# Attention and mixture of experts on one core: router logits in the spare columns of the scores' bank, and other engines for weights and token halves

## The chip, the cores and the metric

The kernel runs on one core of one Trainium2 chip. The metric is the device time of one execution in microseconds (us), and lower is better. A core has a matrix engine (TensorE, "PE" in the rows; "PEld" is its loading of stationary operands), VectorE (DVE), ScalarE (ACT), GpSimd (POOL) and SyncE (SP), which here does nothing but issue transfers. Each engine has its own queue of instructions and works through it in order; a transfer runs on 16 DMA engines that all queues share.

## The reference

Attention inside blocks of 64 tokens makes `x`, 4608 tokens of 512 numbers. Tokens whose skip score is positive go through one of eight experts, the one with the largest logit; the others leave unchanged.

```python
scores = (1 / np.sqrt(D)) * np.matmul(q_c, k_c.transpose(0, 1, 2, 4, 3))   # blocks of 64 tokens
attn = np.exp(scores - scores.max(-1, keepdims=True))
attn = attn / (attn.sum(-1, keepdims=True) + 1e-09)
x = np.matmul(attn, v_c)                       # reordered to (4608, 512)
do_compute = (x @ w_skip) > 0
xc = x[do_compute]
logits = xc @ w_gate                           # 8 experts
e_idx = np.argmax(logits, axis=1)
gate_w = softmax(logits)[e_idx]
for e in range(8):
    h = np.maximum(xc[e_idx == e] @ w1[e], 0.0)        # 512 -> 1024
    y[e_idx == e] = gate_w * (h @ w2[e])               # 1024 -> 512
out = x; out[do_compute] = xc + y
```

## The kernel before, in words

The program has two stages. The first takes 36 tiles of 128 tokens through attention and the router. The second takes the tokens of each expert, gathered from `out`, through the two matrix products of that expert; the expert that is first in the order has its weights loaded and converted already during the first stage, in 16 halves ("pieces") of 128 x 512 numbers.

The first stage is one loop over `i`, and its order is written out by hand: in pass `i` different steps of different tiles stand one behind the other on each engine. On TensorE a pass is: transpose `x` of tile i-3 into the bank `xt` (`pe_xtrans`), transpose the exponentials of tile i-1 (`pt`), subtract the maxima of tile i (`pe_sub`), logits of tile i-4 (`pe_logits`), scores of tile i+1 (`pe_scores`, tile `sp`), product with v of tile i-1 (`pv`). On ScalarE: scale `xt` to `xs` (line 300), copy `pt` to `pts` (257), exponential `px` (245). On VectorE: normalise `pv` to `x` (273 to 277), sum the logits (`lg`, 326), maxima (`mx`, 235), then some steps of the router of a finished group of tiles (`run_route`, groups of 14, 9 and 13 tiles).

Before the logits, `xs` is split into two half-precision parts, the tile `xh`: the high part is a copy (line 302), the low part what the copy left (line 303), both on GpSimd. The logits of a tile are written into columns of the same bank `xt` that `pe_xtrans` of this pass has filled (`rt_bank`, the list `host`), so they come behind the ScalarE step that empties it. For the last five tiles ScalarE and VectorE make `xh` straight from the bank.

`conv_half` converts one piece of weights: ScalarE makes the high part in `wset` (475), GpSimd scales the staged piece `wst` in place (479) and subtracts (480). It is called at the end of a pass, once the piece has been in flight for two passes.

Transfers are issued in bursts. TensorE's instructions are counted, and whenever a block of 256 (`FETCH`) has gone by, SP issues one burst: first `qk` and `v` of tiles up to four ahead, then, until the burst has 6 units (7 from pass `WIDER` on; `qk` counts two, all others one), pieces of weights that `W_TILES` makes due and stores of finished `x` (`held`). A piece or a store is 128 x 512 x 4 bytes, 262,144 bytes.

When the router is through with the first 23 tiles, GpSimd gathers the rows of the first three blocks of the first expert (`early_fetch`, at the end of pass `EARLY_I`). After the loop TensorE finishes the last tiles' logits between the first products of that expert (tile `pd`), and goes on to the second products (`y`) and the other experts.

Of the kernel before, what the change touches and what calls it, by code (L numbers as in the profile page):

```python
# [9 lines left out]
F32 = mybir.dt.float32  # L10
F16 = mybir.dt.float16
# [3 lines left out]
ALU = mybir.AluOpType  # L15
# [3 lines left out]
P = 128  # L19
B, H, S, D = 8, 8, 576, 64  # L20
CH = 64
NTOK = B * S
NT = NTOK // P
DM = H * D
# [3 lines left out]
KC = DM // P  # L28
# [9 lines left out]
GS = (14, 9, 13)  # L38
NG = len(GS)
GT = [(g, i, n) for g, n in enumerate(GS) for i in range(n)]  # L40
EARLY_G, EARLY_B = 2, 3
# [8 lines left out]
FETCH_AT = 193  # L50
FETCH_LAG = 12
BURST = 6
WIDER = 18
W_TILES = (6, 8, 11, 14, 17, 20, 23, 25, 33, 33, 33, 33, 34, 34, 34, 34)
W_ORDER = tuple((fc, part) for part in range(2) for fc in range(FC))
WSETS = 3
STB = 8
# [1 line left out]
XGB = 8  # L59
TLEAD = 2  # L60
XBUFS = 17
EARLY_I = NT - 3

SX = 2.0 ** 6
SW = 2.0 ** 4
# [36 lines left out]
def moe_attention_kernel(ctx: ExitStack, tc: tile.TileContext, qk: bass.AP, v: bass.AP, cst: bass.AP, wall: bass.AP, out: bass.AP):  # L102
    nc = tc.nc
# [7 lines left out]
    ap = apool.__enter__()  # L111
# [3 lines left out]
    ps_s = spool_.__enter__()  # L115
# [4 lines left out]
    T = [dict() for _ in range(NT)]  # L120
# [13 lines left out]
    def mm32(*args, **kw):  # L134
        return issued(nc.tensor.matmul(*args, **kw), 4)  # L135
# [69 lines left out]
    def more_constants():  # L205
        nc.vector.tensor_copy(upper, C("upper"))
        nc.vector.tensor_copy(iota, C("iota"))
        nc.vector.tensor_scalar(wgs[:, :, 0], wg, SR, None, op0=ALU.mult)
        nc.vector.scalar_tensor_tensor(wgs[:, :, 1], wg, SR, wgs[:, :, 0], op0=ALU.mult, op1=ALU.subtract)
        nc.gpsimd.tensor_copy(vals[:, :, 0], C("tok"))  # L210
        nc.gpsimd.tensor_copy(vals[:, :, 2], C("part").to_broadcast([P, NT]))
        nc.gpsimd.memset(ecum[:, 0, :], 0.0)
        nc.gpsimd.memset(rec, 0.0)
# [7 lines left out]

    def pe_scores(t):
        qt = T[t].pop("qk")
        sp = ps_s.tile([P, 2, DM], F32, name="sp")
        for j in range(KC):
            for c in range(2):
                for a in range(2):
                    h = (j % 2) * 4 + (j // 2) * 2 + a
                    w = slice(h * CH, (h + 1) * CH)
                    mm32(sp[halves[a], c, j * CH:(j + 1) * CH], qt[halves[c], 0, w], qt[halves[c], 1, w], start=(j == 0), stop=False, skip_group_check=True)  # L230
        T[t]["sp"] = sp

    def ve_max(t):
        mx = spool.tile([P, H], BF16, name="mx")
# [45 lines left out]
    held = []  # L280
# [11 lines left out]
    def ac_xs(t):  # L292
        if t >= NT - 5:
            T[t]["xh"] = xh = ap.tile([P, 2, KC, P], F16, name="xh")
            xp = T[t].pop("xt")
            nc.scalar.activation(xh[:, 0], xp, AF.Copy, scale=SX)
            nc.vector.scalar_tensor_tensor(xh[:, 1], xp, SX, xh[:, 0], op0=ALU.mult, op1=ALU.subtract)
            return
        xs = ap.tile([P, KC, P], F32, name="xs")
        nc.scalar.activation(xs, T[t].pop("xt"), AF.Copy, scale=SX)  # L300
        T[t]["xh"] = xh = ap.tile([P, 2, KC, P], F16, name="xh")
        nc.gpsimd.tensor_copy(xh[:, 0], xs)  # L302
        nc.gpsimd.tensor_tensor(xh[:, 1], xs, xh[:, 0], op=ALU.subtract)  # L303

    host = []

    def rt_bank():
        if not host:
            host.append(ps_p.tile([P, DM], F32, name="xt"))
        return host[0]  # L310

    def pe_logits(t):
        xh = T[t].pop("xh")
        lp = rt_bank()[:, :2 * NX]
        for j in range(KC):
            mm16(lp, xh[:, 0, j, :], wgs[:, j].rearrange("p z n -> p (z n)"), start=(j == 0), stop=False, skip_group_check=True)
            mm16(lp[:, :NX], xh[:, 1, j, :], wgs[:, j, 0], start=False, stop=(j == KC - 1), skip_group_check=True)
        T[t]["lp"] = lp
# [14 lines left out]
    def route(g):  # L333
# [36 lines left out]

        yield "p", 0
        rk = rt_bank()[:, 32:32 + n * NX]
        mm16(rk, upper, eh.rearrange("p g e -> p (g e)"), start=True, stop=False, skip_group_check=True)
        for i in range(1, n):
# [45 lines left out]
        yield "w", 1  # L420
        yield "p", 0
        rp = rt_bank()[:, 32:32 + 4 * NB]
        for i in range(n):
            mm16(rp, oh[:, i, :], rv[:, i].rearrange("p z b -> p (z b)"), start=(i == 0), stop=(i == n - 1), skip_group_check=True)
# [27 lines left out]
    def run_route(kinds, budget):  # L452
        while routes and routes[0][0][0] in kinds and budget > 0:
            budget -= routes[0][0][1]
            routes[0][0] = next(routes[0][1], None)
            if routes[0][0] is None:
                routes.pop(0)
# [13 lines left out]
    def conv_half(eng=nc.gpsimd):  # L471
        st, fc, r = w_pend.pop(0)
        loaded.pop(0)
        w = wsets[0]
        nc.scalar.activation(w[:, 0, fc, r], st, AF.Copy, scale=SW)
        if eng is nc.vector:
            eng.scalar_tensor_tensor(w[:, 1, fc, r], st, SW, w[:, 0, fc, r], op0=ALU.mult, op1=ALU.subtract)
        else:
            eng.tensor_scalar(st, st, SW, 1.0, op0=ALU.mult, op1=ALU.mult)
            eng.tensor_tensor(w[:, 1, fc, r], st, w[:, 0, fc, r], op=ALU.subtract)  # L480
# [66 lines left out]
    def on(f, t, *a):  # L547
        if 0 <= t < NT:
            f(t, *a)
# [19 lines left out]
    def early_fetch():  # L569
        for m in range(min(EARLY_B, ready[-1])):  # L570
            fetch(m, P * sum(GS[:EARLY_G]))
# [48 lines left out]
    ahead = [f for t in range(4, NT + 1) for f in ([(load_qk, t, 2)] if t < NT else []) + [(load_v, t - 1, 1)]]  # L620
    pieces = list(range(len(W_TILES)))

    def burst(at):
        i, size, put = now[0], 0, []
        while ahead and ahead[0][1] <= i + LOOK and size + ahead[0][2] <= BURST:
            put.append(ahead.pop(0))
            size += put[-1][2]
        while size < BURST + (i >= WIDER):
            if pieces and W_TILES[pieces[0]] <= i:
                put.append((load_half, pieces.pop(0), 1))  # L630
            elif held:
                put.append((store, held.pop(0), 1))
            else:
                break
            size += 1
        for n, (f, t, _) in enumerate(put):
            f(t, None if n else at)

    pe["burst"] = burst
    for i in range(-1, NT):  # L640
        host.clear()
        now[0] = i
        pe["n"] += 1
        run_route("w", 1)
        on(pe_xtrans, i - 3)
        on(ve_norm, i - 2)
        on(ac_xs, i - 3)
        if 0 <= i - 2 < NT:
            held.append(i - 2)
        on(pe_ptrans, i - 1)  # L650
        on(ac_pt, i - 1)
        on(pe_sub, i)
        on(ac_exp, i)
        on(pe_logits, i - 4)
        run_route("p", 1)
        on(ve_logits, i - 4)
        run_route("r", 1)
        on(pe_scores, i + 1)
        on(ve_max, i + 1)
        run_route("d", 750)  # L660
        on(pe_pv, i - 1)
        if i == 1:
            more_constants()
        for _ in range(2 if i == NT - 1 else 1):
            if not w_pend or i < loaded[0] + (2 if i < EARLY_I else 1):
                break
            conv_half()
        while i == EARLY_I and len(ready) == 1:
            host.clear()
            run_route("w", 1)  # L670
            run_route("p", 1)
            run_route("rd", 1 << 30)
        if i == EARLY_I:
            early_fetch()
# [17 lines left out]
    while held:  # L692
        store(held.pop(0))
    store(NT - 2)
    ac_xs(NT - 3)
    pe_logits(NT - 4)
    ve_logits(NT - 4)
# [8 lines left out]
    piece()  # L706
    pe_xtrans(NT - 2, pt_bank)
    ac_xs(NT - 2)
    pe_logits(NT - 3)
    ve_logits(NT - 3)  # L710
# [245 lines left out]
```

## Time and profile before

| | us |
|---|---|
| median of 3 runs (lowest, highest) | 354.51 (353.32, 357.58) |
| the profiled execution | 354.38 |
| its span, first to last instruction | 352.7 |
| TensorE busy | 315.1 (89%) |
| VectorE busy | 237.8 (67%) |
| ScalarE busy | 164.4 (47%) |
| GpSimd busy | 149.2 (42%) |

The mean granted clock of TensorE is 0.982 of 2.4 GHz. The loop over the tiles takes up the first 130 us of the span. The shares are means over both stages; the engines' loads differ much between them, so the sections below read each stage by itself.

### The profile page before, as it was taken

What the parts mean: (1) busy time and instruction counts of PE and PEld (TensorE: products, weight loads), DVE (VectorE), ACT (ScalarE), POOL (GpSimd) and SP (SyncE); (2) the same over time, 40 slices, a digit from 0 to 9 for tenths busy, and PEclk for the clock granted to TensorE, in tenths of its full rate; (3) what the DMA queues carried; (4) which work ended last, traced back from release to release, by engine and by line L of the source; (5) the groups of instructions that cost most, each with busy time, mean ns of one, the idle gap of its engine ahead of it and who ended that gap; (6) DMA issues with size and microseconds to landing.
All of it is one profiled execution on the core that took longest, in us unless ns stands there. A gap on an engine that the chain in (4) does not pass through costs nothing.

```text
span 352.7 us, 11140 instructions
## 1 busy us (share of the span) xinstructions
PE 315.1 (89%) x4543; PEld 222.2 (63%) x4543; DVE 237.8 (67%) x528; ACT 164.4 (47%) x335; POOL 149.2 (42%) x175
## 2 busy tenths in 40 slices
PE   7897979878977868999999998999999999999990
PEld 3786868757856756554655554755756748678570
DVE  1664646797678855875639996975976967778330
ACT  2553645554445365351437633663654644447020
POOL 5263866789748677673200225024214222111111
PEclk9998999998999999999999999999999999999996
DMA  7899799997999899436614597777479578663000
GB/s 291 286 345 329 253 318 308 348 356 264 317 333 334 296 341 318 148 84 239 222 47 160 204 278 245 215 242 239 146 231 288 168 236 274 186 198 108 32 24 30
DMA packets 37430, 81.81 MB, mean 232 GB/s; under 512 B 4590, under 2 KB 4590, under 8 KB 37376
## 3 DMA queue, kind: packets, MB, share of 16 engines
q1 hardware_dynamic: 34128, 71.47, 61.1%
q0 software_dynamic: 3104, 9.33, 8.1%
q8 instruction: 37, 0.61, 0.7%
q10 hardware_dynamic: 144, 0.26, 0.2%
q14 instruction: 17, 0.14, 0.1%
HBM read 67.01 MB, written 14.17 MB: 230 GB/s over the span
## 4 chain that ended last, share of the span: by engine, by line
PE 70%; POOL 8%; DMA 6%; DVE 5%; ACT 4%; issue 3%; SPq 1%; POOLq 0%; ACTq 0%
PE y L533 27%; PE hp L504 21%; PE sp L135 4%; PE xt L138 4%; PE pd L504 4%; DMA wst<-in_wall 4%; PE xt L141 3%; PE pv L135 3%; POOL xh L303 3%; PE xq L496 2%; ACT xs L300 2%; DMA qk<-in_qk 2%; POOL wset L480 2%; POOL rv L406 1%; POOL xh L302 1%
## 5 line engine op out<-in xcount | busy, mean ns | idle before, releaser
L533 PE MATMUL y<-wset,ht 128*128 128x512 f16 (+7 forms) x552 | 101.9, 379 | 0.0
L504 PEld LDWEIGHTS <-wset 128*128 128x128 f16 x864 | 73.5, 98 | 25.8 <-issue 5.5
L483 POOL DMA_INDIRECT out<-yo,reci x22 | 24.7, 1123 | 142.7 <-DVE yo L543 122.6
L504 PE MATMUL hp<-xt,wset 128*128 128x288 f16 (+6 forms) x768 | 80.9, 267 | 1.7 <-DVE ht L509 1.1
L533 PEld LDWEIGHTS <-ht 128*128 128x128 f16 (+7 forms) x552 | 45.6, 101 | 46.5 <-issue 2.0
L768 DVE SCALAR_TENSOR_TENSOR wset<-wst,wset 128x512 f16<-128x512 f32 x112 | 71.5, 683 | 1.4 <-ACT wset L767 0.8
L767 ACT ACTIVATE wset<-wst 128x512 f16<-128x512 f32 x112 | 63.0, 621 | 2.5 <-DMA wst<-in_wall 2.5
L508 ACT ACTIVATE ht<-hp 128x288 f16<-128x288 f32 (+6 forms) x64 | 23.6, 371 | 49.4 <-PE hp L504 49.2
L509 DVE SCALAR_TENSOR_TENSOR ht<-hp,ht 128x288 f16<-128x288 f32 (+6 forms) x64 | 25.4, 406 | 22.6 <-ACT ht L508 21.6
L235 DVE TENSOR_REDUCE mx<-sp 128x8 bf16<-128x512 f32 x36 | 24.8, 690 | 21.4 <-PE sp L135 21.4
L300 ACT ACTIVATE xs<-xt 128x512 f32<-128x512 f32 x31 | 18.4, 595 | 43.4 <-PE xt L141 41.4
L303 POOL TENSOR_TENSOR xh<-xs,xh 128x512 f16<-128x512 f32 x31 | 36.6, 1180 | 2.5
L135 PE MATMUL pv<-v,pts 64*64 64x65 f32 x1152 | 24.8, 221 | 5.4 <-issue 3.6
L497 ACT ACTIVATE xt<-xq 128x512 f16<-128x512 f32 (+7 forms) x19 | 9.6, 509 | 41.8 <-PE xq L496 41.8
L302 POOL CAST xh<-xs 128x512 f16<-128x512 f32 x31 | 19.3, 622 | 22.9 <-ACT xs L300 22.9
L483 POOL DMA_INDIRECT xg<-out,reci x22 | 24.6, 1120 | 7.5 <-issue 4.9
L135 PE MATMUL sp<-qk 64*64 64x64 f32 x1152 | 25.7, 226 | 1.0 <-issue 0.9
L277 DVE TENSOR_TENSOR x<-pv,rr 128x512 f32<-128x512 f32 x36 | 24.9, 692 | 1.2
L141 PE MATMUL xt<-ident,x 128*128 128x128 f32 x132 | 23.2, 296 | 2.6 <-issue 2.6
L543 DVE SCALAR_TENSOR_TENSOR yo<-y,recg,xg 128x512 f32<-128x512 f32 (+7 forms) x23 | 17.1, 743 | 12.3 <-PE y L533 12.1
L135 PEld LDWEIGHTS pv<-v,pts 64*64 64x64 f32 x1152 | 21.0, 136 | 6.3 <-issue 4.3
L138 PEld LDWEIGHTS <-xh 128*128 128x128 f16 x288 | 12.6, 97 | 18.8 <-issue 10.9
(114 smaller groups left out, 365.3 us busy)
## 6 DMA issues: line engine op xcount, KB each, us to landing
wst<-in_wall SPq DMA_DIRECT2D x128, 256.0 KB, 3.9
qk<-in_qk SPq DMA_DIRECT2D x35, 512.0 KB, 5.7
v<-in_v SPq DMA_DIRECT2D x36, 260.0 KB, 5.7
out<-x SPq DMA_DIRECT2D x36, 256.0 KB, 6.1
xg<-out,reci POOLq DMA_INDIRECT x22, 5.3
out<-yo,reci POOLq DMA_INDIRECT x22, 4.3
qk<-in_qk SPq DMA_DIRECT2D x1, 256.0 KB
qk<-in_qk ACTq DMA_DIRECT2D x1, 256.0 KB
```

Of the source, the lines that this page charges most:

```text
L135: return issued(nc.tensor.matmul(*args, **kw), 4)
L138: return issued(nc.tensor.matmul(*args, **kw), 2)
L141: return issued(nc.tensor.transpose(*args), 2)
L277: nc.vector.tensor_tensor(x.rearrange("p (g m d) -> p g m d", g=2, m=KC), pv[:, :, :, :D], rr.unsqueeze(3).to_broadcast([P, 2, KC, D]), op ...
L300: nc.scalar.activation(xs, T[t].pop("xt"), AF.Copy, scale=SX)
L303: nc.gpsimd.tensor_tensor(xh[:, 1], xs, xh[:, 0], op=ALU.subtract)
L483: ins = nc.gpsimd.indirect_dma_start(**kw)
L504: nc.tensor.matmul(hp, w[:, a, fc, j * P:(j + 1) * P], xt[:, b, j, :n], start=(m == 0), stop=(m == 11))
L509: nc.vector.scalar_tensor_tensor(ht[:, 1, fc, :n], hp, 0.0, ht[:, 0, fc, :n], op0=ALU.max, op1=ALU.subtract)
L533: nc.tensor.matmul(y[c * P // cg:c * P // cg + n], ht[:, a, fc, o:o + n], w[:, b, fc, P * KC:], start=(f == 0 and m == 0), stop=(f == fw - ...
L767: nc.scalar.activation(w[:, 0, fc, r], st[part], AF.Copy, scale=SW)
L768: nc.vector.scalar_tensor_tensor(w[:, 1, fc, r], st[part], SW, w[:, 0, fc, r], op0=ALU.mult, op1=ALU.subtract)
```

## The change

Five things are changed.

- The logits of a tile, and the small products of the router, are written into columns 256 to 511 of the first bank of the scores of the tile that comes next (`new_sp` takes that bank ahead of `pe_logits`). The scores use columns 0 to 255. The scores' products now stand ahead of `ve_logits` in the program's text, and behind the logits on TensorE as before.
- From tile 13 on the high part of `xh` is made by ScalarE, behind `pts` and ahead of the exponential; the low part stays on GpSimd.
- In passes below 16 the low part of a piece of weights is made by VectorE in one instruction (line 490 in the changed file) and no longer by GpSimd in two.
- The pieces are due at other passes: the first eight at 4, 7 and 10, the last eight at 30 and 32. Bursts have 7 units from pass 20 on. A store of a tile from 23 on is put only when no piece is left.
- The early gathers stand at the end of pass 32, no longer 33.

```diff
-WIDER = 18
-W_TILES = (6, 8, 11, 14, 17, 20, 23, 25, 33, 33, 33, 33, 34, 34, 34, 34)
+WIDER = 20
+W_TILES = (4, 4, 4, 7, 7, 7, 10, 10, 30, 30, 30, 32, 32, 32, 32, 32)
+W_VE = 16
+HI_ACT = 13
-EARLY_I = NT - 3
+EARLY_I = NT - 4
     def pe_scores(t):
...
-        sp = ps_s.tile([P, 2, DM], F32, name="sp")
+        sp = T[t]["sp"]
...
     def ac_xs(t):
...
-        T[t]["xh"] = xh = ap.tile([P, 2, KC, P], F16, name="xh")
-        nc.gpsimd.tensor_copy(xh[:, 0], xs)
-        nc.gpsimd.tensor_tensor(xh[:, 1], xs, xh[:, 0], op=ALU.subtract)
+        T[t]["xs"] = xs
+        if t < HI_ACT:
+            xh_of(t, nc.gpsimd.tensor_copy)
+
+    def xh_of(t, copy):
+        xs = T[t].pop("xs", None)
+        if xs is not None:
+            T[t]["xh"] = xh = ap.tile([P, 2, KC, P], F16, name="xh")
+            copy(xh[:, 0], xs)
+            nc.gpsimd.tensor_tensor(xh[:, 1], xs, xh[:, 0], op=ALU.subtract)
...
+    def new_sp(t):
+
+        T[t]["sp"] = sp = ps_s.tile([P, 2, DM], F32, name="sp")
+        host.append(sp[:, 0, KC * CH:])
...
-            elif held:
+            elif held and (held[0] < sum(GS[:EARLY_G]) or not pieces):
                 put.append((store, held.pop(0), 1))
...
+        on(xh_of, i - 3, nc.scalar.copy)
         on(pe_sub, i)
         on(ac_exp, i)
+        on(new_sp, i + 1)
         on(pe_logits, i - 4)
         run_route("p", 1)
+        on(pe_scores, i + 1)
         on(ve_logits, i - 4)
         run_route("r", 1)
-        on(pe_scores, i + 1)
         on(ve_max, i + 1)
...
-            conv_half()
+            conv_half(nc.vector if i < W_VE else nc.gpsimd)
```

TensorE in one pass of the loop, from the last logits to the product with v. Before:

```order
L138 MATMUL xt<-wgs,xh 128x18
L138 LDWEIGHTS xh
L138 MATMUL xt<-wgs,xh 128x9
L135 MATMUL sp<-qk 64x64 x16
L135 MATMUL pv<-v,pts 64x65 x16
```

And now:

```order
L140 MATMUL sp<-wgs,xh 128x18
L140 LDWEIGHTS xh
L140 MATMUL sp<-wgs,xh 128x9
L137 MATMUL sp<-qk 64x64 x16
L137 MATMUL pv<-v,pts 64x65 x16
```

The order is the same; the logits' target is now the scores' tile.

GpSimd while the router handles its first group, around tile 20. Here `rv` are products for the router's sums. Before:

```order
L406 TENSOR_TENSOR rv<-ohb,vals 128x264
L479 TENSOR_SCALAR wst<-wst 128x512
L480 TENSOR_TENSOR wset<-wst,wset 128x512
L302 CAST xh<-xs 128x512
L303 TENSOR_TENSOR xh<-xs,xh 128x512
L406 TENSOR_TENSOR rv<-ohb,vals 128x264 x2
```

And now:

```order
L382 TENSOR_TENSOR vals<-gate,vals 128x14
L311 TENSOR_TENSOR xh<-xs,xh 128x512
L419 TENSOR_TENSOR rv<-ohb,vals 128x264
L311 TENSOR_TENSOR xh<-xs,xh 128x512
L419 TENSOR_TENSOR rv<-ohb,vals 128x264 x2
```

The two instructions on weights and the cast of the high part are gone from this queue.

VectorE in a pass from 6 to 13. Before:

```order
L273 TENSOR_SCALAR rs<-pv 128x8
L275 RECIPROCAL rr<-rs 128x8
L277 TENSOR_TENSOR x<-pv,rr 128x512
L326 TENSOR_REDUCE lg<-xt 128x9
L235 TENSOR_REDUCE mx<-sp 128x8
```

And now:

```order
L274 TENSOR_SCALAR rs<-pv 128x8
L276 RECIPROCAL rr<-rs 128x8
L278 TENSOR_TENSOR x<-pv,rr 128x512
L339 TENSOR_REDUCE lg<-sp 128x9
L236 TENSOR_REDUCE mx<-sp 128x8
L490 SCALAR_TENSOR_TENSOR wset<-wst,wset 128x512
```

One instruction on weights follows the maxima in each of eight passes.

GpSimd at the end of the loop, around the early gathers. Before:

```order
L302 CAST xh<-xs 128x512
L303 TENSOR_TENSOR xh<-xs,xh 128x512
L483 DMA xg<-out,reci 128x512 x3
L479 TENSOR_SCALAR wst<-wst 128x512
L480 TENSOR_TENSOR wset<-wst,wset 128x512
```

And now:

```order
L311 TENSOR_TENSOR xh<-xs,xh 128x512 x2
L492 TENSOR_SCALAR wst<-wst 128x512
L493 TENSOR_TENSOR wset<-wst,wset 128x512
L496 DMA xg<-out,reci 128x512 x3
L311 TENSOR_TENSOR xh<-xs,xh 128x512
```

Before, the gathers follow the last `xh` (tile 30) and precede the weights; now one piece of weights and the three gathers precede that last `xh`.

## Rows read from the trace of the kernel before

**Rows 1.** Busy time by engine in four stretches of the program, the loop first

```profile
core 0: us, PE busy (x) PEld busy (x) DVE busy (x) ACT busy (x) POOL busy (x), PEclk, DMA share, GB/s
19.00:118.60 99.60, 81.97 (x2296) 71.07 (x2285) 67.59 (x188) 48.65 (x93) 69.65 (x84) 0.97 0.93 319
...
118.60:134.80 16.20, 12.51 (x344) 10.74 (x341) 11.30 (x29) 9.84 (x20) 11.97 (x13) 1.00 0.91 306
134.80:154.30 19.50, 18.43 (x155) 11.96 (x155) 14.08 (x39) 7.06 (x15) 13.93 (x15) 1.00 0.51 176
154.30:352.70 198.40, 186.84 (x1399) 117.93 (x1396) 136.79 (x254) 91.42 (x196) 45.07 (x41) 0.99 0.58 182
```

**Rows 2.** The same for an undisturbed tile, 5 us, and four router tiles

```profile
20.83:23.62 2.79, 2.68 (x86) 2.39 (x83) 1.83 (x5) 1.58 (x4) 1.77 (x3) 1.00 1.00 335
...
65.00:70.00 5.00, 4.84 (x132) 4.13 (x132) 3.54 (x11) 1.78 (x4) 4.67 (x7) 1.00 0.98 361
...
71.16:88.68 17.52, 13.38 (x346) 11.56 (x343) 14.16 (x36) 8.12 (x15) 15.74 (x21) 0.90 0.86 306
```

**Rows 3.** TensorE in order of time: start, duration, instruction (undisturbed tile)

```profile
20.83 0.69 PE L135 MATMUL sp<-qk 64*64 64x64 f32 x32
...
22.85 0.38 PE L138 MATMUL sp<-mx,identb 128*128 128x256 bf16 x2
23.34 0.34 PE L138 MATMUL xt<-wgs,xh 128*128 128x18 f16 x8
23.62 0.29 PE L135 MATMUL sp<-qk 64*64 64x64 f32 x4
```

**Rows 4.** ScalarE in order of time, the same tile

```profile
22.70 0.60 ACT L300 ACTIVATE xs<-xt 128x512 f32<-128x512 f32 x1 [1.21 <-PE xt L141]
...
23.67 0.60 ACT L245 ACTIVATE px<-sp 128x512 f32<-128x512 f32 x1
```

**Rows 5.** TensorE's waits, 65.3 to 118.6 us: total us, times, longest

```profile
PE xt L138 <- POOL xh L303: 2.6, 3, 1.2
PE xt L141 <- issue: 2.6, 2, 1.8
PE pv L135 <- issue: 1.6, 2, 1.0
PE xt L138 <- ACT xs L300: 1.2, 2, 0.7
...
PE xt L138 <- POOL xh L302: 0.6, 2, 0.3
```

**Rows 6.** TensorE's waits, 19 to 65.3 us

```profile
PE pv L135 <- issue: 2.0, 1, 2.0
PE xt L138 <- ACT xs L300: 1.9, 2, 1.0
```

**Rows 7.** GpSimd in order of time, router's first group

```profile
69.68 1.16 POOL L303 TENSOR_TENSOR xh<-xs,xh 128x512 f16<-128x512 f32 x1
...
75.40 0.62 POOL L479 TENSOR_SCALAR wst<-wst 128x512 f32<-128x512 f32 x1
76.10 1.16 POOL L480 TENSOR_TENSOR wset<-wst,wset 128x512 f16<-128x512 f32 x1
```

**Rows 8.** VectorE in order of time, the same instruction in two groups

```profile
69.72 1.15 DVE L365 SCALAR_TENSOR_TENSOR den<-den,fixed 128x14 f32<-128x14 f32 x1
...
103.02 0.17 DVE L365 SCALAR_TENSOR_TENSOR den<-den,fixed 128x9 f32<-128x9 f32 x1
```

**Rows 9.** TensorE in order of time, the loop's last logits

```profile
124.75 0.34 PE L138 MATMUL xt<-wgs,xh 128*128 128x18 f16 x8 [0.81 <-DVE xh L297]
...
129.78 0.34 PE L138 MATMUL xt<-wgs,xh 128*128 128x18 f16 x8 [2.10 <-DVE xh L297]
```

**Rows 10.** GpSimd in order of time, the early gathers

```profile
123.29 1.26 POOL L483 DMA_INDIRECT xg<-out,reci  x1 [0.17 <-DVE rr L275]
...
126.19 1.01 POOL L483 DMA_INDIRECT xg<-out,reci  x1 [0.30 <-issue]
```

**Rows 11.** Groups by line: busy us, mean ns (second stage's conversion on VectorE)

```profile
L768 DVE SCALAR_TENSOR_TENSOR wset<-wst,wset 128x512 f16<-128x512 f32 x112 | 71.5, 683 | 1.4 <-ACT wset L767 0.8
```

More of the change, by code (lines that the diff above doesn't have):

```diff
@@ L230, in pe_scores @@
                     mm32(sp[halves[a], c, j * CH:(j + 1) * CH], qt[halves[c], 0, w], qt[halves[c], 1, w], start=(j == 0), stop=False, skip_group_check=True)
-        T[t]["sp"] = sp
     def ve_max(t):
```

## The prediction

> **What bounds the kernel now.** I read busy time by stretches first, then one undisturbed tile on each engine, then what TensorE waited for. The stretches [rows 1] separate two regimes. From 134.8 us on TensorE is busy nearly all the time (18.43 of 19.50 us, then 186.84 of 198.40), and the change touches nothing in that part; I move it as a block. In the loop over the tiles, 19 to 118.6 us, TensorE is busy 81.97 of 99.60 us, and no compute engine is full: VectorE 67.59, ScalarE 48.65, GpSimd 69.65. What is nearly full are the DMA engines: 0.93 of the time, at 319 GB/s, so 99.6 x 319 = 31.8 MB move there. At a share of 1.00 that takes 0.93 x 99.6 = 92.6 us, a rate of 343 GB/s. This is the number that I build on: the loop has 7.0 us to give before the transfers alone set its length, however many waits vanish.
>
> An undisturbed tile takes 2.79 us, with VectorE busy 1.83, ScalarE 1.58, GpSimd 1.77 [rows 2]. Its TensorE rows show one small gap: `pe_sub` starts at 22.85 and takes 0.38, the logits start at 23.34 [rows 3], just after `xs` has left the bank (22.70 + 0.60 = 23.30) [rows 4].
>
> What TensorE waits for has two kinds. For other engines: `xh` from GpSimd 2.6 + 0.6, `xs` 1.2 in the later half [rows 5], `xs` 1.9 in the earlier one [rows 6]; together 6.3 us. And for "issue", which here is its own next block of instructions, fetched by the same DMA engines that carry the bursts: 2.6 + 1.6 [rows 5] and 2.0 [rows 6].
>
> **The change part by part.**
>
> *Logits beside the scores.* TensorE's order stays. What goes is the wait for `xs`: the gap is 23.34 - (22.85 + 0.38) = 0.11 us at the least. Instructions in a row overlap, so more is possible, up to the whole time from the logits' start to that of the next scores, 23.62 - 23.34 = 0.28. That is 0.11 to 0.28 us in each of some 28 tiles, 3.1 to 7.8 us, if nothing else is late. The new wait is for the scores' bank, freed by the exponential of an earlier pass; the scores waited for the same before, so it costs nothing. VectorE's `lg` now comes when the scores are through, 0.5 us later, ahead of the maxima that wait for the scores anyway: nothing.
>
> *High halves by ScalarE, 18 tiles.* The cast leaves GpSimd and adds one copy of 0.60 [rows 4] to ScalarE, 1.58 + 0.60 = 2.18 us a tile, under any pace that the transfers allow. The queue behind it holds the exponential, 0.5 us later. The low half comes later too: copy in the place of `px`, 23.67 to 24.27, then 1.16 on GpSimd [rows 4, 7], so it ends 1.9 us after the scores' start at 23.62, or 2.2 when the scores no longer wait. The next logits come 2.2 us after that start in the shortest tile and 2.7 at the transfers' pace: cost 0, at worst 0.3 x 18 = 5 us if the transfers did not hold the pace.
>
> *First weights by VectorE, passes 6 to 13.* GpSimd loses 0.62 + 1.16 [rows 7] eight times, 14 us, and the stalls behind it. VectorE gains eight instructions like those of the second stage, 0.683 each [rows 11]: 1.83 + 0.68 = 2.51 us in those tiles. They have two operands in SBUF, and such an instruction took 1.15 us instead of 0.17 [rows 8] when it met GpSimd's subtraction, which ran from 69.68 to 70.84 [rows 7]; so each may cost up to 1.16 more, 3.67 in the tile. I take 0.2, since the maxima end about where the low half ends. The Trainium skill, "GPSIMD Engine Reference", section 8 (Key points), states the rule: GpSimd shares its SBUF interfaces with VectorE, and instructions with two SBUF inputs contend. The rows above agree with it; it speaks against this edit, and is weighed as a rival.
>
> *Router tiles.* From 71.16 to 88.68 GpSimd was busy 15.74 of 17.52 us [rows 2]. Without two pieces and five casts some 6 us of it go. Next is VectorE, 14.16 us in the same stretch, so at most 3.4 us can be won there.
>
> *Bursts.* They are full before and after, and a burst of 6 units is 1.57 MB, 4.6 us at 343 GB/s; only which unit goes when changes. Up to the pass of the last `qk` two transfers fewer are issued (the step to 7 units comes two passes later, and the burst with the pieces of pass 30 has 6): 0.52 MB, 1.5 us. Stores fall back to some 13 tiles behind, and `x` has 17 buffers, so nobody waits. Eight stores come after the loop, with DMA only half busy there [rows 1]: nothing.
>
> *Sum of the loop.* (92.6 - 1.5) / share. With 1.00: 91.1, with 0.93: 98.0. The share was 0.93 with the stalls, in the stretch of TensorE's longest stall for GpSimd only 0.86 [rows 2]. I take 0.97, because waits for the fetched block remain: 93.9 us, **-5.7 us** (between -8.5 and -1.6).
>
> *The end of the loop.* Here something is added. GpSimd now has, behind the low half of tile 29, a piece of weights and three gathers ahead of the low half of tile 30, which the logits in pass 34 need. From the start of the scores in pass 32: low half 2.2, piece 0.7 + 1.2 = 4.1, gathers 123.29 to 127.20 = 3.9 [rows 10], so 8.0, low half 1.2: 9.3 us. TensorE wants it after two tiles less 0.28, 4.7 to 5.5 us: a stall of 3.8 to 4.6 us. In return the two waits there go, 0.81 and 2.10 us [rows 9]; the second comes from ScalarE being held by a piece still in flight, and the pieces now come earlier. With 0.3 us for shorter tiles: **+1.0 us** (from -3.4, no stall, to +4.6, stall and old waits).
>
> *Behind the loop* the order is the same, with the eight stores and an earlier end of the conversion: 0, at most 1 us either way.
>
> Sum: -5.7 + 1.0 = -4.7. The profiled execution took 354.38 us (span 352.7 and 1.7 around it), the median is 354.51, so there is nothing to correct: 354.38 - 4.7 = **349.7 us**, 1.3% less.
>
> **The rivals.**
>
> *A. Transfers set the pace, as above:* 349.7, by itself 346.5 to 353.
>
> *B. They do not; all waits for other engines turn into time.* For it: for 5 us the DMA engines moved 361 GB/s [rows 2]. Then the loop gives 6.3 us of waits and the middle of 3.1 to 7.8, 5.5: -11.8, and +1.0 at the end: 343.6 us. The loop would move 31.3 MB in 87.8 us, 356 GB/s all the way, just under that rate. Against: the blocks of instructions are fetched through the same engines, and a faster TensorE meets the bursts' remains earlier. The Trainium skill, "DMA: Bandwidth & Descriptors", section "Queues, rings and completion order", says that each DMA engine goes round between its queues packet by packet; by that a fetch would not stand behind a whole burst, and the time would be B's. The row of a 2.0 us wait for issue [rows 6] does not look like it.
>
> *C. Nothing that can be measured.* Either the share stays at 0.93, -1.6 + 1.0, 353.8 us; or VectorE is held by GpSimd in the eight passes, 3.67 us instead of the 3.07 that 1.05 MB a tile take at 343 GB/s: 0.6 x 8 = 4.8 us, and 349.7 + 4.8 = 354.5. This is also the case of the rule on the shared interfaces taken in full. I put it at 354. For it: the 1.15 us [rows 8]. Against: the maxima end when the low half is nearly done, and 3.07 - 2.51 leaves 0.56 us of slack.
>
> *D. Slower: the end of the loop.* The one place where the change puts work ahead of something on TensorE's path. If the stall is 4.6 us, the old waits stay, because ScalarE is held by the new pieces' landing, and the loop gains only 1.6, the time is 354.38 + 4.6 - 1.6 = 357.4. It decides from the point where the stall's excess over the 2.9 us that go is more than the loop's gain.
>
> **How the numbers follow.** A 0.50, B 0.20, C 0.20, D 0.10. The forecast is A's time. The range holds 8 in 10: from B's time to C's upper price, with half a us for B and one for C's unknown, 343.0 to 355.5; outside lie half of B's spread and D. This kernel's measurement tells about 2% from no change, 7.1 us: under 347.4 lie B and a fifth of A, 0.30; above 361.6 only a bad D, 0.03; the rest 0.67.
>
> **What would show it.** Right: DMA share of 0.96 to 0.98 in the loop, the last scores 3 to 6 us earlier, GpSimd no longer among TensorE's waits before pass 33, more waits for issue than 6 us, and one wait for `xh` of about 4 us at the last tiles. The second stage's length stays within 1 us of 218. Wrong: a rate over 350 GB/s over the whole loop (B), VectorE's new instructions of over 1.2 us each (C), or a stall at the end over 5 us (D). What I trust least is the price of the waits for instructions, which no row shows at a faster pace.

## The result and the profile after

| | before | after |
|---|---|---|
| median of 15 runs each, side by side (lowest, highest), us | 355.63 (353.32, 359.2) | 352.82 (348.91, 355.64) |
| profiled execution, its span, us | 354.38, 352.7 | 353.22, 351.5 |
| mean granted clock | 0.982 | 0.977 |

The ratio is 0.9888, with a 95% interval of 0.986 to 0.9917: faster by about 1.1%, less than 2%. (It is taken over undisturbed runs alone, so it is not quite that of the medians.) The forecast of 349.7 is 0.986 of the 354.51 that it started from, at the interval's lower edge; the changed kernel's median is 3 us above it.

The first fence has stretches of the changed kernel, as in [rows 1, 2]: the loop between the same two bursts as before, the end of the loop up to the first `pd` product, the second stage behind its first block, and one undisturbed tile.

```profile
core 0: us, PE busy (x) PEld busy (x) DVE busy (x) ACT busy (x) POOL busy (x), PEclk, DMA share, GB/s
20.56:113.59 93.03, 78.15 (x2292) 71.31 (x2284) 69.18 (x196) 56.54 (x109) 46.17 (x51) 0.98 0.96 334
113.59:132.76 19.17, 13.93 (x345) 12.42 (x342) 11.37 (x30) 12.19 (x24) 14.53 (x15) 0.91 0.93 321
...
152.90:351.50 198.60, 187.48 (x1393) 117.78 (x1391) 136.01 (x252) 90.38 (x195) 43.82 (x40) 0.98 0.56 181
32.07:34.61 2.54, 2.54 (x86) 2.41 (x83) 1.91 (x6) 2.09 (x5) 1.77 (x2) 1.00 0.87 296
```

The loop takes 93.0 us instead of 99.6 [rows 1] (99.54 between exactly the same bursts, 19.03 to 118.57), the undisturbed tile 2.54 instead of 2.79 [rows 2], and the end of the loop 19.2 instead of 16.2 (16.27) at a lower granted clock, 0.91 instead of 1.00. The loop starts 1.5 us later in this execution (20.56 against 19.03; in the traces of this document it starts anywhere from 18.1 to 21.3), and from the first `pd` product to the end it is 218.7 us (351.5 - 132.76) instead of 217.9 (352.7 - 134.8). Sum: 1.5 - 6.5 + 2.9 + 0.8 = -1.3 us, the difference of the two spans within rounding.

TensorE's waits in that loop (total us, times, longest), the answer to [rows 5, 6]:

```profile
PE pv L137 <- ACT px L246: 4.7, 6, 1.5
PE pt L143 <- ACT xs L301: 2.1, 2, 1.2
PE pv L137 <- DVE mx L236: 1.8, 1, 1.8
PE pv L137 <- issue: 1.7, 3, 1.4
PE pv L137 <- ACT xh L310: 1.6, 3, 0.8
PE sp L137 <- issue: 1.4, 3, 0.7
PE pv L137 <- ACT pts L258: 0.8, 1, 0.8
PE pt L143 <- issue: 0.7, 1, 0.7
```

GpSimd has gone from the list, and `xh` is waited for only as ScalarE's copy. Waits for issue are 3.8 us here; but the sum of all waits, 14.8 us, is hardly below the 15.4 that the same view of the kernel before adds up to. ScalarE has taken GpSimd's place. How, its own rows in order of time show for the longest of these waits (start, duration, instruction), and then TensorE's next row:

```profile
27.52 0.63 ACT L488 ACTIVATE wset<-wst 128x512 f16<-128x512 f32 x1 [1.97 <-DMA wst<-in_wall]
28.05 0.58 ACT L301 ACTIVATE xs<-xt 128x512 f32<-128x512 f32 x1
28.53 0.59 ACT L258 ACTIVATE pts<-pt 128x512 f32<-128x512 f32 x1
29.01 0.60 ACT L246 ACTIVATE px<-sp 128x512 f32<-128x512 f32 x1
```

```profile
30.01 0.70 PE L137 MATMUL pv<-v,pts 64*64 64x65 f32 x32 [1.54 <-ACT px L246]
```

ScalarE stood 1.97 us at a piece of weights that had not landed; `xs`, `pts` and the exponential queued behind it, and TensorE behind them. It stood so three times in the loop (1.97, 1.27 and 0.48 us), and each time TensorE then waited for `px` (1.54, 0.94 and 0.38): 2.9 of the 4.7 us. The other waits for `px`, 0.3 to 0.8 us each, follow no such piece.

The end of the loop, TensorE and GpSimd in order of time, answers to [rows 9, 10]:

```profile
119.27 0.17 PE L140 MATMUL sp<-wgs,xh 128*128 128x18 f16 x1
123.02 0.33 PE L140 MATMUL sp<-wgs,xh 128*128 128x9 f16 x7 [3.58 <-POOL xh L311]
123.28 1.04 PE L137 MATMUL sp<-qk 64*64 64x64 f32 x32
124.07 1.11 PE L137 MATMUL pv<-v,pts 64*64 64x65 f32 x32
```

```profile
117.87 1.26 POOL L496 DMA_INDIRECT xg<-out,reci  x1 [0.17 <-DMA v<-in_v]
119.44 1.02 POOL L496 DMA_INDIRECT xg<-out,reci  x1 [0.31 <-PE pt L143]
120.76 1.01 POOL L496 DMA_INDIRECT xg<-out,reci  x1 [0.30 <-issue]
121.79 1.17 POOL L311 TENSOR_TENSOR xh<-xs,xh 128x512 f16<-128x512 f32 x1
```

The logits of tile 30 wait 3.58 us for their low half, which stands behind the three gathers. The scores behind the wait take 1.04 us instead of 0.69: from 123 to 127 us the granted clock was 0.57, near the lower of TensorE's two levels, after the 3.58 us in which it had stood.

VectorE's conversion, its group by line (busy us, mean ns, idle time before it), answers to [rows 11]:

```profile
L490 DVE SCALAR_TENSOR_TENSOR wset<-wst,wset 128x512 f16<-128x512 f32 x8 | 5.9, 737 | 3.2 <-ACT wset L488 3.2
```

Each lasted 681 to 931 ns. Six took 0.68 to 0.69 us; the two longest, 0.93 and 0.84, began 0.4 and 0.3 us before GpSimd's subtraction for a low half ended.

### The profile page after: what moved, and what is told of

Same layout as the page of the kernel before. It is cut to its first block, busy times and chain, and to the rows that moved or that the text cites. A ratio compares the mean times of both kernels' runs of the same rounds, so it can differ in the third digit from the quotient of the medians.

```text
span 351.5 us, 11129 instructions
## 1 busy us (share of the span) xinstructions
PE 315.0 (90%) x4543; PEld 225.7 (64%) x4543; DVE 238.7 (68%) x536; ACT 173.7 (49%) x353; POOL 124.0 (35%) x141
## 4 chain that ended last, share of the span: by engine, by line
PE 58%; DVE 4%; ACT 1%; DMA 1%; issue 1%; POOL 1%; POOLq 0%; DVEq 0%; ACTq 0%
PE y L546 28%; PE hp L517 21%; PE pd L517 4%; PE xq L509 2%; DMA xg<-out,reci 1%; DVE wset L783 1%; PE pt L143 1%; DVE yo L556 1%; PE sp L137 1%; PE pv L137 1%; PE xt L140 1%; POOL xg L496 1%; DVE xt L511 1%; PE xt L143 0%; DVE xh L298 0%
## 5 line engine op out<-in xcount | busy, mean ns | idle before, releaser
L546 PE MATMUL y<-wset,ht 128*128 128x512 f16 (+7 forms) x552 | 103.6, 383 | 0.0
L137 PE MATMUL pv<-v,pts 64*64 64x65 f32 x1152 | 25.7, 224 | 12.6 <-ACT px L246 4.7
L137 PEld LDWEIGHTS pv<-v,pts 64*64 64x64 f32 x1152 | 21.7, 137 | 14.6 <-issue 6.4
L137 PE MATMUL sp<-qk 64*64 64x64 f32 x1152 | 27.1, 231 | 1.9 <-issue 1.4
L143 PE MATMUL pt<-ident,px 128*128 128x128 f32 x144 | 23.4, 286 | 2.8 <-ACT xs L301 2.1
L137 PEld LDWEIGHTS sp<-qk 64*64 64x64 f32 x1152 | 21.7, 140 | 4.8 <-issue 2.0
L258 ACT ACTIVATE pts<-pt 128x512 f32<-128x512 f32 x36 | 21.3, 593 | 6.4 <-PE pt L143 5.7
```

Source lines behind the costliest of these rows:

```text
L143: return issued(nc.tensor.transpose(*args), 2)
L546: nc.tensor.matmul(y[c * P // cg:c * P // cg + n], ht[:, a, fc, o:o + n], w[:, b, fc, P * KC:], start=(f == 0 and m == 0), stop=(f == fw - ...
```

## The experiments

All ratios are against the kernel before, run beside it; the median of before was 355.8 to 356.4 us in the three sets.

**The end of the loop: later gathers.** Gathers at the end of pass 33, as in the kernel before.

```diff
-        if i == EARLY_I:
+        if i == EARLY_I + 1:
             early_fetch()
```

> The changed kernel, with the three early gathers at the end of pass 33 again (behind the low half of tile 30); all else as changed. Theory (the gathers in front of that low half cost a stall of 3.6 us and slow TensorE after it): the stall is gone, the time is 2.5 to 4 us under the changed kernel's, ratio to before 0.978 to 0.982. Rival (the stall is cover for something that is late next, as the gathered rows or ScalarE's pieces): same as the changed kernel within 1 us, ratio 0.986 to 0.991, with another wait of 2 to 4 us between the last scores and the first pd product.

Measured: 352.01 us, 0.9885 (0.983 to 0.9939), the time of the changed kernel. The 3.58 us wait is gone, but the stretch from the last burst to the first `pd` product is 19.0 us, as long as in the changed kernel (114.36 to 133.39), at a DMA share of 0.99. TensorE in order of time:

```profile
128.03 0.66 PE L509 MATMUL pd<-ident,xg 128*128 128x128 f32 x4 [1.67 <-DMA xg<-out,reci]
...
130.34 2.36 PE L509 MATMUL pd<-ident,xg 128*128 128x128 f32 x8 [1.03 <-DMA xg<-out,reci]
```

The later gathers are themselves late, 2.7 us in two waits.

**The end of the loop: GpSimd off the path.** Tile 30's `xh` straight from the bank, gathers early.

```diff
-        if t >= NT - 5:
+        if t >= NT - 6:
```

> The changed kernel, with tile 30's halves made by ScalarE and VectorE straight from the bank, as for the last five tiles; the gathers stay in pass 32. Theory (GpSimd's queue at the gathers is the cause): the stall of 3.6 us is gone, 2.5 to 4 us under the changed kernel, ratio to before 0.978 to 0.982. Rival (something else is late next there): within 1 us of the changed kernel, ratio 0.986 to 0.991.

Measured: 352.78 us, 0.9898 (0.986 to 0.9935), again no gain. No wait for GpSimd; but TensorE, in order of time, at the same place:

```profile
120.60 0.81 PE L137 MATMUL sp<-qk 64*64 64x64 f32 x15
121.83 0.34 PE L137 MATMUL sp<-qk 64*64 64x64 f32 x3 [0.43 <-issue]
122.58 0.31 PE L137 MATMUL sp<-qk 64*64 64x64 f32 x3 [0.40 <-issue]
123.36 0.69 PE L137 MATMUL sp<-qk 64*64 64x64 f32 x11 [0.47 <-issue]
```

The scores get their instructions a few at a time and are through at 124.0 instead of about 121.3. From 120 to 125 us the granted clock was 0.84 and the DMA share 0.95. In the changed kernel TensorE stood at the wait for GpSimd in just these microseconds, so such a wait would be hidden there; that it was there too is inferred.

**The last stores out of the way.** The 13 stores of the last tiles wait until the second expert's first eight weight loads have been issued, and these loads move forward (first issue at 121.8 and 119.9 us instead of 133.3); with tile 30's `xh` as in the changed kernel, and as in the run above.

```diff
-            elif held and (held[0] < sum(GS[:EARLY_G]) or not pieces):
+            elif held and held[0] < sum(GS[:EARLY_G]):
...
-    while held:
-        store(held.pop(0))
-    store(NT - 2)
     ac_xs(NT - 3)
...
-    store(NT - 1)
     feed_load()
+    while held:
+        store(held.pop(0))
+    store(NT - 2)
+    store(NT - 1)
```

> The changed kernel with its last 13 stores of x issued behind the first eight weight pieces of the second expert, so from about 135 us on, and no longer from 118.8 us. Theory (the end of the loop is paced by transfers as well: 6.1 MB go there in 19.2 us at a share of 0.93, 3.4 MB of them these stores, and TensorE's blocks of instructions come through the same engines): the stretch from the last burst with qk to the first pd product shrinks from 19.2 to 16 to 17 us, held now by the 3.6 us wait for tile 30's xh alone, and the time is 1 to 3 us less than the changed kernel's, ratio 0.980 to 0.987 against before. Rival (the order of the engines sets the end; the stores only fill idle DMA time): the stretch stays 19 us, ratio 0.987 to 0.991, or more if the gathers of the second stage at 150.7 us now wait for the stores.

> As the run with the late stores, and tile 30's xh made straight from the bank, so that GpSimd is off TensorE's path at the end. With early stores and that xh the 3.6 us wait had gone, but the scores of tile 34 were cut up by waits for issue at the same place, 120.6 to 124.0 us, and the stretch was 18.1 us long. Theory (those waits are TensorE's instructions fetched through full DMA engines): with the 3.4 MB of stores out of the way the pieces of 0.4 us disappear and the stretch is 14.5 to 15.5 us, 3 to 4 us less than in that run; time 349 to 350 us, ratio 0.976 to 0.982. Rival (waits for issue come whatever the DMA engines do): the same pieces at the same place, stretch 18 us, ratio 0.987 to 0.991.

Measured: late stores alone 354.0 us, 0.9946 (0.9905 to 0.9988); with tile 30's `xh` from the bank 347.82 us, 0.9777 (0.9724 to 0.9831), less than the changed kernel by 5.0 us in the medians and by 1.1% in the ratios, and faster than with either edit alone. Late stores alone leave the wait for GpSimd (2.95 us) and a granted clock of 0.83 over the stretch: my expectation of 16 to 17 us for the stretch failed, it was 19.7. With both, TensorE at the same place, and the end of the loop by stretch:

```profile
120.40 0.35 PE L140 MATMUL sp<-wgs,xh 128*128 128x18 f16 x8
120.67 0.69 PE L137 MATMUL sp<-qk 64*64 64x64 f32 x32
121.19 0.65 PE L137 MATMUL pv<-v,pts 64*64 64x65 f32 x32
```

```profile
114.72:129.30 14.58, 12.62 (x344) 11.06 (x341) 11.72 (x31) 11.78 (x23) 12.07 (x13) 1.00 0.84 278
```

No wait for issue in the scores, no wait for GpSimd, the granted clock at 1.00, 14.6 us instead of 19.2. Either edit alone gave nothing; both together take 4.6 us off this stretch. In the two profiled executions the rest nearly cancels: the loop is 2.2 us longer than the changed kernel's, the part behind the first `pd` product 2.2 us shorter (216.5 instead of 218.7), the start 1.0 us earlier.

What the scores waited for with the early stores is not shown by this. The DMA engines were as full with both edits (share 0.99 from 119 to 123 us, now with weight loads in the place of stores). Like series, a few matmuls between waits of 0.3 to 0.5 us, stand in two more traces at the product with v, that of the logits alone (121.4 to 123.6 us) and that of the kernel before with `q` alone (118.3 to 119.8), where SP issued one store at that time and not 13. In all three traces the early gathers run beside them; with the later gathers, and 13 early stores, the scores at the same place took 0.69 us (120.32). So the stores alone do not make the series, nor do the gathers alone; what does stays open.

**More to transfer.** One load more in each burst from pass 4 to 31, 18 in all, into a tile that nobody reads.

```diff
+        if 4 <= i <= 31:
+            put.append((load_extra, 0, 1))
...
+    def load_extra(m, at=None):
+        paced(nc.sync.dma_start(ep.tile([P, DM], F32, name="ex2"), wall[ORDER[1], 0, :, 0:DM]), at)
```

> The changed kernel with one load more (128 x 512 x 4 bytes of weights into a tile that nobody reads) at the end of each burst from pass 4 to 31, about 18 loads, 4.7 MB; no engine but SP and the DMA engines has more to do. Theory (transfers set the loop's pace): 4.7 MB at 343 GB/s are 13.8 us, the changed loop has 0.04 x 93 = 3.7 us of unused share, so the loop is 9 to 13 us longer and the ratio against before 1.015 to 1.025. Rival (the engines' waits for each other set the pace, the share is high only because bursts are issued early): the loads fill the unused 3.7 us first and shift little, 0 to 3 us, ratio 0.989 to 0.997.

> The kernel before with the same 18 loads more. Theory (transfers set the pace, with the stalls on top): unused share 0.07 x 99.5 = 7.0 us, so 13.8 - 7.0 = 7 us at the least and 12 at most if the stalls stay; ratio 1.020 to 1.034, and the loop has the same length within 2 us as that of the changed kernel with the loads, since the change's gain is then gone. Rival (engine waits set the pace): 0 to 3 us, ratio 1.000 to 1.008, and the change's gain of 1.1% stays between the two kernels with the loads.

Measured: 356.81 us, 1.0006 (0.9962 to 1.0049), on top of the change, 4.0 us more than without the loads; 359.21 us, 1.0083 (1.0046 to 1.0119), on the kernel before. The loops, first with the change and then without:

```profile
20.09:117.68 97.59, 76.88 (x2292) 69.95 (x2284) 69.30 (x196) 56.26 (x109) 45.76 (x51) 1.00 1.01 363
```

```profile
20.67:119.20 98.53, 81.53 (x2292) 70.22 (x2284) 66.71 (x187) 48.55 (x93) 69.27 (x83) 0.98 1.01 359
```

The loads cost far less than the 9 to 13 and 7 to 12 us of the theory, and the engines moved 363 and 359 GB/s over the whole loop: 343 is no ceiling. Nor does the rival hold throughout: with the change the loop is 4.6 us longer than in the changed kernel's trace and its waits for issue are 10.1 us instead of 3.8, and of the 6.5 us between the two loops 0.9 are left. But on the kernel before the loop is 1.0 us shorter with the loads than without, and its waits for issue stay (7.9 against 8.0 us); and in the whole time 2.4 us of the change's 2.8 are left between the medians, much as the rival said.

**Less to transfer.** Only `q` is loaded and used as `k` too.

```diff
-        paced(nc.sync.dma_start(T[t]["qk"], qk[t]), at)
+        paced(nc.sync.dma_start(T[t]["qk"][:, 0], qk[t][:, 0]), at)
...
-    ... qt[halves[c], 0, w], qt[halves[c], 1, w], ...
+    ... qt[halves[c], 0, w], qt[halves[c], 0, w], ...
```

> The changed kernel with only the q half of each tile loaded, and q used in the place of k: 256 KB less per tile, about 7.3 of the loop's 31.1 MB, the same instructions on TensorE, VectorE, ScalarE and GpSimd. The scores, and with them the routing, are other numbers, so only the loop over the tiles is read. Theory (full DMA engines lengthen the loop through what waits behind the bursts: blocks of TensorE's instructions and pieces of weights that land late): waits for issue in the loop fall from 3.8 us in the changed kernel to under 1.5, ScalarE's waits for a piece vanish and with them most of the 4.7 us of waits for px, and the loop takes 85 to 89 us instead of 93 to 96. Rival (the engines' own order and a fixed price of each block of instructions set it): waits stay, 91 to 95 us.

> The kernel before with only the q half loaded, as in the run beside it. Theory: the waits for issue go (7.4 us in the loop), those for xs and for xh from GpSimd stay (3.1 + 3.5 us): loop 92 to 95 us instead of 99.5, and 5 to 8 us longer than that of the changed kernel with the q half alone: without the transfers the change's gain is larger. Rival (the engines' own order): 96 to 100 us, and the difference between the two stays 4 to 6 us.

The routing differs, so the whole time says nothing; each of the two kernels was run once. The loop with the change, and TensorE's waits in it for issue and for `px`:

```profile
18.05:103.69 85.64, 76.24 (x2293) 70.08 (x2284) 69.20 (x194) 56.27 (x109) 45.74 (x51) 1.00 0.86 277
```

```profile
PE pv L137 <- ACT px L245: 4.2, 6, 1.6
PE pt L143 <- issue: 1.2, 2, 0.8
...
PE pv L137 <- issue: 0.5, 2, 0.3
...
PE xt L143 <- issue: 0.2, 1, 0.2
```

And without the change:

```profile
18.80:110.70 91.90, 79.75 (x2292) 69.63 (x2284) 67.28 (x188) 48.16 (x93) 69.75 (x84) 0.98 0.83 267
```

```profile
PE xt L138 <- POOL xh L302: 3.8, 6, 1.2
PE xt L138 <- ACT xs L299: 3.0, 4, 1.1
PE pv L135 <- issue: 0.8, 1, 0.8
```

Some 7.3 MB less shorten both loops by 7.4 and 7.6 us, and the waits for issue in the loop fall from 3.8 to 1.9 and from 8.0 to 0.8: they hang on what else the DMA engines move. All of TensorE's waits together fall by 5.7 us in both. The change is worth 6.3 us between these two loops, no more than the 6.5 with all transfers: the rival's figure was 4 to 6, the theory's 5 to 8. The waits for `px` do not vanish as expected (4.2 of 4.7): ScalarE waits for pieces here too, up to 1.14 us.

**The parts by themselves.** The logits' move alone on the kernel before, and all the rest without it (the lines with `new_sp` and the place of `pe_scores`, as in the change's diff):

```diff
+        on(new_sp, i + 1)
         on(pe_logits, i - 4)
         run_route("p", 1)
+        on(pe_scores, i + 1)
         on(ve_logits, i - 4)
         run_route("r", 1)
-        on(pe_scores, i + 1)
```

> The kernel before, with only the logits moved beside the next tile's scores. Theory (transfers and GpSimd set the loop's pace): undisturbed tiles take 2.54 instead of 2.79 us, but the loop gives only 0 to 2.5 us, ratio 0.993 to 1.000. Rival (the wait for xs is worth its 0.25 us in every tile): 6 to 7 us, ratio 0.98 to 0.983.

> The changed kernel with the logits back in the bank xt; weights, high halves, bursts and gathers as changed. Theory (transfers set the pace, so the logits' place hardly matters): within 2.5 us of the changed kernel, ratio to before 0.988 to 0.996. Rival (the logits' place is the gain): the whole gain goes, ratio 0.998 to 1.006.

Measured: logits alone 355.4 us, 0.9955 (0.9914 to 0.9996); all the rest 353.31 us, 0.9952 (0.9918 to 0.9986). Somewhat under half of the gain each, with intervals as wide as the halves. In the trace of the logits alone GpSimd's `xh` is waited for 5.9 us in the loop, more than the 3.5 of the kernel before: the logits now come before the low half is ready.

```diff
-HI_ACT = 13
+HI_ACT = 99
```

```diff
-W_VE = 16
+W_VE = 0
```

> The changed kernel with the high half of xh made by GpSimd in all tiles up to 30, as before the change. Theory (the casts are what GpSimd could not carry beside the router): waits for xh from GpSimd come back in the router tiles and at the end, where five operations stand behind the gathers, 1 to 4 us, ratio 0.992 to 1.000. Rival (the copy on ScalarE delays the exponential and the product with v by as much, 4.7 us of waits for px in the changed kernel's trace): ratio 0.982 to 0.990, waits for px down to under 2 us.

> The changed kernel with the first eight pieces converted by GpSimd again, at the changed passes. Theory (GpSimd with 1.77 us for xh and 1.78 us for a piece, 3.55 us in a tile of 2.6 to 3.1 us, holds the logits in passes 6 to 13): waits for xh of 3 to 6 us there, ratio 0.996 to 1.006. Rival (only the due passes matter, since the router does not run yet in these passes; the queue of GpSimd catches up in the free tiles between the groups of pieces): 0 to 1 us, ratio 0.987 to 0.992.

Measured: high halves on GpSimd again 353.54 us, 0.988 (0.9829 to 0.9932); first pieces on GpSimd again 355.41 us, 0.9966 (0.9928 to 1.0005). TensorE's largest wait in the loop, of the one and of the other:

```profile
PE pv L137 <- ACT px L246: 7.9, 10, 1.4
```

```profile
PE sp L140 <- POOL xh L311: 6.9, 8, 1.1
```

The copy on ScalarE is worth nothing either way; the waits for `px` rose without it, so it is not their cause, and GpSimd's `xh` is waited for only at the end (2.9 and 1.0 us). The pieces on VectorE are worth 2.6 us in the medians: without them the logits wait for GpSimd in eight tiles, from 32.5 to 58.6 us, about 1.05 us in six of them.

## Why the prediction was right, and where it was not

**The loop, -5.7 us.** Measured -6.5 in the profiled execution. The four variants with the same loop took 95.7, 94.9, 96.2 and 95.2 us; with the changed kernel's 93.0 the mean is 95.0, -4.5 against the one trace of the kernel before. The size holds. Its ground does not, so that it holds is in part luck: "the loop has 7.0 us to give before the transfers alone set its length" fell when 363 GB/s went through the loop. At that rate the changed loop's 31.1 MB take 86 us, not 92.6 - 1.5.

What the traces show in its place is a sum. Taking all of TensorE's waits off the loop leaves 84.1 us before, and 83.6, 84.0 and 82.2 in the three other traces with the logits in `xt`; with the logits beside the scores it is 78.2, and 76.5 to 79.7 in the nine others. So the logits' move takes some 5.5 us off the time between waits, in the middle of the 3.1 to 7.8 that the prediction allowed; the clock, 0.95 to 1.00 in these loops, is not taken out. And with the kernel's own transfers the waits add up to 13 to 18 us whatever the change: GpSimd's go, ScalarE's come, and those for issue vary from 3.0 to 8.8 (0.8 and 1.9 us with 7.3 MB less). The trace of the logits alone has a loop of 94.7 us, 4.8 less than before; but it is of that kernel's fastest run (350.9 us, median 355.4), and over all its runs the gain is 0.45%, 1.6 us. That the transfers take back part of the gain, as the forecast had it, is not shown: the two loops differ by 6.3 us with 7.3 MB less, and by 6.5, or 4.5 from the mean, with all of them.

**The end of the loop, +1.0 us.** This term was mis-sized: it measured +2.9. The place and the mechanism were right: a wait of 3.58 us (3.8 to 4.6 forecast) for tile 30's low half behind a piece and three gathers, and of the two old waits, 0.81 and 2.10 us, one of 0.44 is left. Two things were left out. Behind the wait TensorE ran at a granted clock of 0.57 (0.91 over the stretch, instead of 1.00): scores and product with v took 1.04 and 1.11 us instead of 0.69 and 0.65, and from the scores' start to the next `pe_sub` it was 3.60 us (123.28 to 126.88) instead of 2.14 a tile earlier, 1.5 us more. And removing the wait alone gave nothing: in one variant the scores at this place then took 2.8 us longer, cut up by waits for issue, in the other the gathers came late. The prediction put the stores at nothing: "Eight stores come after the loop, with DMA only half busy there". SP issued 13 of them from 118.8 to 133.2 us, within the end of the loop, at a DMA share of 0.93; only with these moved as well did the stretch shrink. Two of the prediction's additions are off: the terms up to the low half make 9.2 us and not 9.3, and the bound without a stall is -3.2 and not -3.4; the forecast does not change by it.

**The other steps.** Right: the second stage within 1 us of 218; DMA share 0.96; GpSimd gone from TensorE's waits in the loop; the ScalarE copies at no cost in the whole time. VectorE's instructions took 737 ns on average, 0.05 us above [rows 11], where the prediction took 0.2 and rival C up to 1.16 more. The Trainium skill, "GPSIMD Engine Reference", section 8 (Key points), has GpSimd contend with VectorE instructions that have two SBUF inputs; the two of eight that met a subtraction of GpSimd's, 0.93 and 0.84 us, agree with it, at a price of 0.4 us in all. Wrong: the last scores came 1.7 us earlier (123.28 against 125.02) and not 3 to 6; and more than 6 us of waits for issue in the loop were 3.8 in this trace, though 6.7 to 8.8 in the four variants. (Before they were 8.0; the lines of [rows 5, 6] show 6.2 of them.) The waits for ScalarE held by a piece in flight were named for the end of the loop and not for its early passes, where they now cost up to 1.54 us.

**The rivals.** B's time is 9 us off; that 350 GB/s could be passed was right, that all waits would turn into time was not. The Trainium skill, "DMA: Bandwidth & Descriptors", section "Queues, rings and completion order", has each DMA engine go round between its queues packet by packet; a fetch would then not stand behind a whole burst. That does not by itself cover what is seen here: the waits for issue fell from 8.0 to 0.8 us with fewer bytes. How the packets of a fetch and of a burst alternate, no run shows. C's 354 is nearer to the median than A's 349.7 (1.2 against 3.1 us), but the median of the kernel before was 1.1 us higher beside it than in the prediction, and by the ratio the time is 350.5 (0.9888 x 354.51), nearer to A; and a ratio of 1 lies outside the interval. Of C's mechanisms the share did not stay at 0.93, and VectorE was held for 0.4 us and not for 4.8. D's stall came; it cost less than the loop gave.

## What to carry to other kernels

A share of DMA time near 1 does not give the largest rate: test it with loads that nobody reads before a floor is computed from it. Where a visible wait is removed and the time stays, look at the same microseconds of the new trace, for another wait may have lain under it or come in its place; here two edits had to go together before the stretch shrank, by 4.6 us. An instruction that waits for a transfer on an in-order queue is to be placed by what stands behind it on that engine.

## What the runs showed of the hardware

Waits for issue come in two forms, single ones of up to 2.9 us (in the loop of the run with the late stores) and series of 0.4 us with a few matmuls between (above, from 120.6 us). The blocks of instructions are a DMA queue of their own in the view of the queues (packets, MB, share) of the changed loop:

```profile
q8 instruction: 18, 0.29, 1.2%
```

That is 18 packets in 93 us and under 1% of the bytes. TensorE ran 2292 matmuls and 2284 loads of weights there, 254 instructions to a packet, which fits blocks of 256. The waits for issue cost it 3.8 us in this loop, and 10.1 in that with the loads that nobody reads, with 18 packets as well. The series do not fit whole blocks, as only three to five matmuls lie between two waits; what they wait for is not shown. At a DMA share of 0.93 to 1.01 the rate of the loops lay between 316 and 363 GB/s, so the share tells little about what room is left.
